# Where the high and low parts of the second weights stay before they are stored

## The chip, the cores and the metric

The kernel runs on one core of a Trainium2 chip. The metric is the device time of one execution in microseconds. Three runs of the kernel before took 868.1 us in the median, from 867.8 to 869.28.

## The reference

A retention layer (4 batches, 8 heads, 576 positions, head size 64) is followed by two MLPs on 2304 tokens of width 512, with 2048 hidden units each. The first has softplus, the second x * sigmoid(1.702 x). The MLP weights come as float64.

```python
ret = (q @ k.T / 8 * decay) @ v                  # per batch and head, causal
x = ret.transpose(0, 2, 1, 3).reshape(2304, 512)
x = softplus(x @ moe_w_in) @ moe_w_out
h = x @ moe2_w_in
out = (h * sigmoid(1.702 * h)) @ moe2_w_out
```

## The kernel before

**Precision.** Each float32 operand of a matmul is split into a high part (a cast to float32r) and a low part (the operand minus the high part). A product is three matmuls: high by high, low by high, high by low.

**Stages.** The work list of the first MLP runs over five token blocks (three batches of 512 tokens, a block "t" of the four batches' last 64 tokens each, and the last batch) and, in each, over 16 hidden blocks of 128. Between its matmuls `run_first` calls `side()`. Each call advances two Python generators by a rate: the retention of the next batch (`batch`) and one conversion of weights. So every engine's order of instructions is fixed when the program is built. The first weights are converted beside the first batch (`w1_gen`). From the second block on the generator is `w2_gen` at `W2RATE` 1.1, which converts the second MLP's weights in 32 pieces of 128 x 512 and stores them to DRAM. At the start of block "t" what is left of it is run out (L1108), the pools of that stage are closed, and `sums_steps` reads the whole weights back to build sums of quarters. In the second MLP (`run_second`, a seven-product scheme of Strassen-Winograd) the weights are loaded again as high and low halves from the DRAM tiles `kept_d`, `rest_d` and `sums_d`.

**One conversion step** (`convert`, L101). A weight arrives as two 32-bit words. ACT rescales the high word as a float into a tile `wa` (L110, "rebase"); VectorE keeps the sign (L115) and puts the bits together in two shift-or instructions (L130, L137); ACT casts the high part (L141 by the helper at L93); VectorE subtracts for the low part (L146 by the helper at L98). A `yield` stands between these, so each piece falls behind another matmul group in the queues. `begin(i)` for the second weights issues the read of piece i+2 on SP's queue (L576); `end(i, a)` is `w2_store`: it stores the two parts on SP's queue (L600) to one or two DRAM places, and the whole float piece on the GpSimd queue (L602). Then the next piece is rebased.

**Buffers.** The pool `wr` has two buffers of `wa` (4 KB per partition; the second weights use the first half) and three of the tag `raw64` (4 KB each), shared by the raw pieces that are read and by the `halves` tile:

```python
t = wr.tile([P, DM, 2], U32, tag="raw64", name="raw64", bufs=3)            # w2_read
w2_half["t"] = wr.tile([P, 2, DM], F32R, tag="raw64", name="halves", bufs=3)  # w2_place
```

A tile's buffer comes free when all its readers are done, a store from it included; the instruction that first writes the next tile in that buffer waits for that. Which free buffer a tile gets is settled when the program is built.

**SP's queue** holds, in the order of the program, the loads of k, q, v (L302) and of the ends (L306), the reads L576 and the stores L600. A DMA that waits holds up those behind it.

Of the kernel before, what the change touches and what calls it, by code (L numbers as in the profile page):

```python
# [7 lines left out]
F32 = mybir.dt.float32  # L8
F32R = mybir.dt.float32r
# [6 lines left out]
P = 128  # L16
# [9 lines left out]
N2 = 256  # L26
# [3 lines left out]
KEPT = [("in", "11"), ("in", "12"), ("in", "22"), ("out", "11"), ("out", "21"), ("out", "22")]  # L30
# [3 lines left out]
def kernel(  # L34
# [35 lines left out]
    nc = tc.nc  # L70
    B, _, NPAIR, _, KQV = kqv.shape
    H, D = 2 * NPAIR, P // 2
    NT, DM = out.shape
# [14 lines left out]
    def f32(t):  # L88
        return t.bitcast(F32)

    def hi(eng, dst, src):
        if eng == "a":
            nc.scalar.copy(dst, src)  # L93
        else:
            nc.vector.tensor_copy(dst, src)

    def lo(dst, src, h):
        nc.vector.tensor_tensor(out=dst, in0=src, in1=f32(h), op=ALU.subtract)  # L98


    def convert(n, ready, words, place, begin, end, early):  # L101

        def rebase(i):
            w = words(i)
            a = wr.tile([P, 2 * DM], F32, tag="wa", name="wa")[:, 0:w.shape[1]]
            nc.scalar.mul(a, w[:, :, 1].bitcast(F32), 2.0 ** -112)  # L110
            return w, a

        def sign(w):
            high = w[:, :, 1]
            nc.vector.tensor_single_scalar(out=high, in_=high, scalar=0x80000000, op=ALU.bitwise_and)  # L115

        nxt = None
        signed = set()
        for i in range(n):
            while nxt is None:  # L120
                if ready(i):
                    nxt = rebase(i)
                yield
            w, a = nxt
            nxt = None
            u = a.bitcast(U32)
            low, high = w[:, :, 0], w[:, :, 1]
            if i not in signed:
                sign(w)
            nc.vector.scalar_tensor_tensor(  # L130
                out=u, in0=u, scalar=3, in1=high, op0=ALU.logical_shift_left, op1=ALU.bitwise_or)
            begin(i)
            ahead = i + 1 < n and early(i + 1) and ready(i + 1)
            if ahead:
                nxt = rebase(i + 1)
            yield
            nc.vector.scalar_tensor_tensor(  # L137
                out=u, in0=low, scalar=29, in1=u, op0=ALU.logical_shift_right, op1=ALU.bitwise_or)
            yield
            h, l = place(i)  # L140
            hi("a", h, a)  # L141
            if ahead:
                sign(nxt[0])
                signed.add(i + 1)
            yield
            lo(l, a, h)  # L146
            end(i, a)
            if nxt is None and i + 1 < n and ready(i + 1):
                nxt = rebase(i + 1)
            yield  # L150

    def w_tile():
        return wp.tile([P, 2, 2, DM], F32R, tag="w", name="w")
# [87 lines left out]
    with tc.manual_schedule():  # L241
# [6 lines left out]
        kept_d = [dp.tile([P, 2, 4, N2], F32R, tag=f"kept_{i}", name=f"kept_{i}") for i in range(6 * NP // 4)]  # L248
        sums_d = {(j, s): dp.tile([P, 2, 4, N2], F32R, tag=f"sums_{s}{j}", name=f"sums_{s}{j}")
                  for j in range(NP) for s in ("in", "out")}  # L250
        rest_d = {(j, s): dp.tile([P, 2, 4, N2], F32R, tag=f"rest_{s}{j}", name=f"rest_{s}{j}")
                  for j in range(NP // 4) for s in ("in", "out")}
# [27 lines left out]
        with ExitStack() as consts, ExitStack() as right, ExitStack() as second:  # L280
            ac = consts.enter_context(tc.tile_pool(name="ac", bufs=1))
            ap = right.enter_context(tc.tile_pool(name="ap", bufs=2, side="right"))
            wr = right.enter_context(tc.tile_pool(name="wr", bufs=2, side="right"))
# [12 lines left out]
            halves = [slice(h * D, (h + 1) * D) for h in range(2)]  # L296
# [226 lines left out]
            for sv in svs[0] + svs[1]:  # L523
# [3 lines left out]
                out=mask[:, 0:4, :].rearrange("p (t u) j -> p t (u j)", u=2),  # L527
                in_=mask[:, 0:4, :].rearrange("p (t u) j -> p t (u j)", u=2), compare_op=ALU.is_ge, fill=0.0,
# [15 lines left out]

            made = {"f": 0}

            def w1_place(f):
                w1[f] = w_tile()
                return [w1[f][:, i].rearrange("p s n -> p (s n)") for i in range(2)]

            w1_gen = convert(
                NF, lambda f: (1, f) in raws, lambda f: raws.pop((1, f)), w1_place, lambda f: None,
                lambda f, a: made.update(f=f + 1), lambda f: f > 1)

# [24 lines left out]

            w2_half = {}  # L580

            def w2_place(i):
                w2_half["t"] = wr.tile([P, 2, DM], F32R, tag="raw64", name="halves", bufs=3)
                return w2_half["t"][:, 0], w2_half["t"][:, 1]

            def w2_store(i, a):

                j, o, s = i // 4, i // 2 % 2, ("in", "out")[i % 2]
                t = w2_half["t"].rearrange("p h (c n) -> p h c n", c=2)
                names = [(s, f"{o + 1}{n + 1}") for n in range(2)]  # L590
                n = 0
                while n < 2:
                    m = 1
                    if names[n] in KEPT:
                        m = 2 if n == 0 and names[1] in KEPT else 1
                        q = 6 * j + KEPT.index(names[n])
                        dst = kept_d[q // 4][:, :, q % 4:q % 4 + m, :]
                    else:
                        dst = rest_d[j // 4, s][:, :, j % 4:j % 4 + 1, :]
                    nc.sync.dma_start(out=f32(dst), in_=f32(t[:, :, n:n + m, :]))  # L600
                    n += m
                nc.gpsimd.dma_start(out=whole_d[j, s][:, o, :], in_=a)  # L602

            def w2_steps():

                w2_read(0)
                w2_read(1)
                for _ in range(8):
                    yield
                yield from convert(  # L610
                    2 * NF, lambda i: (2, i) in raws, lambda i: raws.pop((2, i)), w2_place,
                    lambda i: w2_read(i + 2), w2_store, lambda i: False)
# [601 lines left out]
```

## Time and profile before

| | |
|---|---|
| median of three runs | 868.1 us (867.8 to 869.28) |
| the profiled execution's own time | 867.41 us |
| its span | 865.7 us |
| TensorE busy | 847.3 us (98%) |
| VectorE busy | 577.5 us (67%) |
| ACT busy | 408.4 us (47%) |
| GpSimd busy | 97.1 us (11%) |
| mean busy share of the DMA queues of SP / GpSimd | 36.8% / 33.6% of 16 engines |

The times of matmuls are modelled and overlap, so a busy TensorE is not one at its peak. Waits are put down to the event that came last. A DMA's landing time counts from its issue.

### The profile page before, as it was taken

Reading aid. Unit: us, or ns where it says so; the run is one execution under the profiler, and the core shown is the slowest. Engines: PE = TensorE matmul, PEld = TensorE weight load, DVE = VectorE, ACT = ScalarE, POOL = GpSimd, SP = SyncE. Lnnn points to the kernel's source line nnn. Section 1 sums busy time; section 2 is a strip of 40 time slices with the busy share of each in tenths; the row PEclk is TensorE's granted clock in tenths of the full one; section 3 lists DMA queues with packets and bytes.
Section 4 is the critical chain, followed back from the end, with each engine's and each line's share of the span. In section 5 each row is a group of like instructions: output and inputs, shape, how many; then the busy total and the mean of one; then the engine's idle time right before and its main releaser. Section 6 shows DMA issues by size and latency. Waiting matters only on the chain.

```text
span 865.7 us, 15675 instructions
## 1 busy us (share of the span) xinstructions
PE 847.3 (98%) x6155; PEld 760.0 (88%) x6155; DVE 577.5 (67%) x1162; ACT 408.4 (47%) x809; POOL 97.1 (11%) x174
## 2 busy tenths in 40 slices
PE   8899999999999999999999999999999999999997
PEld 5678888888878778999888899999999999999997
DVE  5899964767567765577433467788778777866521
ACT  4655544344354433456333455465555555554321
POOL 4100001100110000101001121100011111001000
PEclk9999999999999999999999999999999999999999
DMA  9836531777869776599996596978697779776511
GB/s 362 346 130 219 210 110 62 231 273 268 287 227 300 244 234 237 209 368 334 384 368 209 180 348 240 319 297 291 243 319 282 262 265 336 270 262 223 204 68 25
DMA packets 62777, 217.30 MB, mean 251 GB/s; under 512 B 6384, under 2 KB 20848, under 8 KB 50416
## 3 DMA queue, kind: packets, MB, share of 16 engines
q1 hardware_dynamic: 45136, 111.96, 36.8%
q0 software_dynamic: 17568, 104.34, 33.6%
q8 instruction: 48, 0.79, 0.3%
q14 instruction: 25, 0.20, 0.1%
HBM read 157.56 MB, written 58.72 MB: 250 GB/s over the span
## 4 chain that ended last, share of the span: by engine, by line
PE 62%; issue 19%; DVE 9%; DMA 5%; ACT 3%; POOL 2%; POOLq 0%; SPq 0%; DVEq 0%; ACTq 0%
PE ph L765 15%; PE m L765 14%; PE ph L162 13%; PE y L162 12%; DMA kept<-halves 3%; PE y L765 3%; PE ps_h L331 2%; DMA xo<-x 1%; PE ps_s L383 1%; DVE wa L137 1%; POOL w L684 1%; DVE wa L130 1%; PE ps_y L331 1%; DVE w L98 1%; DMA sums_out<-sum_halves 1%
## 5 line engine op out<-in xcount | busy, mean ns | idle before, releaser
L162 PE MATMUL y<-gh,w 128*128 128x512 f32 (+1 forms) x640 | 196.6, 371 | 0.0
L162 PE MATMUL ph<-xh,w 128*128 128x512 f32 (+1 forms) x640 | 185.8, 374 | 5.3 <-ACT xh L93 2.0
L162 PEld LDWEIGHTS ph<-xh,w 128*128 128x128 f32 x640 | 115.3, 190 | 29.0 <-ACT xh L93 2.4
L162 PEld LDWEIGHTS y<-gh,w 128*128 128x128 f32 x640 | 117.1, 189 | 21.0
L162 PE MATMUL ph<-xl,w 128*128 128x512 f32 (+1 forms) x320 | 118.6, 371 | 0.2 <-DVE xl L98 0.2
L162 PE MATMUL y<-gl,w 128*128 128x512 f32 (+1 forms) x320 | 117.8, 368 | 0.0
L765 PE MATMUL m<-w,ga 128*128 128x256 f32 x768 | 117.3, 282 | 0.5 <-DVE yb L837 0.5
L98 DVE TENSOR_TENSOR gl<-g,gh 128x512 fp32r<-128x512 f32 (+1 forms) x80 | 51.0, 637 | 90.3 <-ACT gh L93 89.9
L765 PE MATMUL ph<-xo,w 128*128 128x256 f32 x768 | 105.8, 283 | 2.5 <-DVE ho L1031 1.1
L765 PE MATMUL ph<-xo_c,w 128*128 128x256 f32 x768 | 108.3, 283 | 0.0
L765 PEld LDWEIGHTS m<-w,ga 128*128 128x128 f32 x768 | 102.8, 190 | 1.1 <-PE ph L765 1.1
L765 PEld LDWEIGHTS ph<-xo,w 128*128 128x128 f32 x768 | 97.6, 189 | 4.1 <-DVE ho L1031 2.2
L765 PEld LDWEIGHTS ph<-xo_c,w 128*128 128x128 f32 x768 | 97.9, 188 | 1.4 <-DVE he L993 0.6
L210 ACT ACTIVATE g<-ph 128x512 f32<-128x512 f32 (+1 forms) x80 | 44.3, 553 | 115.0 <-PE ph L162 111.9
L765 PE MATMUL m<-w,gb 128*128 128x256 f32 x576 | 89.7, 282 | 0.0
L765 PEld LDWEIGHTS m<-w,gb 128*128 128x128 f32 x576 | 78.1, 191 | 0.0
L162 PEld LDWEIGHTS ph<-xl,w 128*128 128x128 f32 x320 | 60.8, 190 | 11.1 <-DVE xl L98 0.8
L162 PEld LDWEIGHTS y<-gl,w 128*128 128x128 f32 x320 | 60.4, 189 | 9.3
L93 ACT CAST halves<-wa 128x512 fp32r<-128x512 f32 x32 | 19.8, 619 | 78.8 <-DMA kept<-halves 31.5
L98 DVE TENSOR_TENSOR ga<-g,ga 128x512 fp32r<-128x512 f32 x72 | 47.0, 685 | 10.0 <-ACT ga L93 10.0
L93 ACT CAST ga<-g 128x512 fp32r<-128x512 f32 x72 | 44.7, 621 | 16.2 <-PE y L765 7.9
L93 ACT CAST gh<-g 128x512 fp32r<-128x512 f32 (+1 forms) x80 | 46.3, 578 | 2.4
(153 smaller groups left out, 1144.9 us busy)
## 6 DMA issues: line engine op xcount, KB each, us to landing
w<-sums_in POOLq DMA_DIRECT2D x32, 1024.0 KB, 5.6
w<-sums_out POOLq DMA_DIRECT2D x32, 1024.0 KB, 7.8
raw<-kqv SPq DMA_DIRECT2D x24, 512.0 KB, 4.5
w<-kept POOLq DMA_DIRECT2D x12, 1024.0 KB, 8.2
w_raw<-w_in SPq DMA_DIRECT2D x16, 512.0 KB, 7.0
w_raw<-w_out SPq DMA_DIRECT2D x16, 512.0 KB, 7.8
raw<-w_in SPq DMA_DIRECT2D x16, 512.0 KB, 4.5
raw<-w_out SPq DMA_DIRECT2D x16, 512.0 KB, 4.2
```

Of the source, the lines that this page charges most:

```text
L93: nc.scalar.copy(dst, src)
L98: nc.vector.tensor_tensor(out=dst, in0=src, in1=f32(h), op=ALU.subtract)
L130: nc.vector.scalar_tensor_tensor(out=u, in0=u, scalar=3, in1=high, op0=ALU.logical_shift_left, op1=ALU.bitwise_or)
L137: nc.vector.scalar_tensor_tensor(out=u, in0=low, scalar=29, in1=u, op0=ALU.logical_shift_right, op1=ALU.bitwise_or)
L162: nc.tensor.matmul(out_ap, l, r, start=first and i == 0, stop=last and i == k - 1)
L210: nc.scalar.activation(g, ph, AF.Softplus)
L331: nc.tensor.matmul(po[halves[h], at], l, rhs, start=clear[h], stop=True, skip_group_check=True)
L383: nc.tensor.matmul(ps[h][:, j], k[r, j], q[r, j], start=True, stop=True)
L684: nc.gpsimd.dma_start(out=where[i], in_=src)
L765: nc.tensor.matmul(out_ap, l, r, start=clear, stop=True, skip_group_check=True)
```

## The change

Three things change, all in the conversion of the second weights. The cast writes the high part into the second half of the piece's own `wa` tile. The low part is written over the first half of the raw piece, whose words have all been read by then. So there is no `halves` tile, and the three `raw64` buffers hold raw pieces only. High and low are then in two tiles, so `w2_store` issues its stores for each of them; the DRAM places stay as they were. The first weights' `w1_place` gets the new arguments and ignores them.

```diff
         def rebase(i):
             w = words(i)
-            a = wr.tile([P, 2 * DM], F32, tag="wa", name="wa")[:, 0:w.shape[1]]
-            nc.scalar.mul(a, w[:, :, 1].bitcast(F32), 2.0 ** -112)
-            return w, a
+            t = wr.tile([P, 2 * DM], F32, tag="wa", name="wa")
+            nc.scalar.mul(t[:, 0:w.shape[1]], w[:, :, 1].bitcast(F32), 2.0 ** -112)
+            return w, t
...
-            w, a = nxt
+            w, t = nxt
             nxt = None
+            a = t[:, 0:w.shape[1]]
...
-            h, l = place(i)
+            h, l = place(i, w, t)
...
-            def w1_place(f):
+            def w1_place(f, w, t):
...
-            def w2_place(i):
-                w2_half["t"] = wr.tile([P, 2, DM], F32R, tag="raw64", name="halves", bufs=3)
-                return w2_half["t"][:, 0], w2_half["t"][:, 1]
+            def w2_place(i, w, t):
+                w2_half["t"] = (t[:, DM:2 * DM].bitcast(F32R),
+                                w.rearrange("p n two -> p (n two)")[:, 0:DM].bitcast(F32R))
+                return w2_half["t"]
 
             def w2_store(i, a):
...
-                t = w2_half["t"].rearrange("p h (c n) -> p h c n", c=2)
                 names = [(s, f"{o + 1}{n + 1}") for n in range(2)]
-                n = 0
-                while n < 2:
-                    m = 1
-                    if names[n] in KEPT:
-                        m = 2 if n == 0 and names[1] in KEPT else 1
-                        q = 6 * j + KEPT.index(names[n])
-                        dst = kept_d[q // 4][:, :, q % 4:q % 4 + m, :]
-                    else:
-                        dst = rest_d[j // 4, s][:, :, j % 4:j % 4 + 1, :]
-                    nc.sync.dma_start(out=f32(dst), in_=f32(t[:, :, n:n + m, :]))
-                    n += m
+                for part, t in enumerate(w2_half["t"]):
+                    n = 0
+                    while n < 2:
+                        m = 1
+                        if names[n] in KEPT:
+                            m = 2 if n == 0 and names[1] in KEPT else 1
+                            q = 6 * j + KEPT.index(names[n])
+                            dst = kept_d[q // 4][:, part, q % 4:q % 4 + m, :]
+                        else:
+                            dst = rest_d[j // 4, s][:, part, j % 4:j % 4 + 1, :]
+                        nc.sync.dma_start(
+                            out=f32(dst), in_=f32(t[:, n * N2:(n + m) * N2]).rearrange("p (c n) -> p c n", c=m))
+                        n += m
                 nc.gpsimd.dma_start(out=whole_d[j, s][:, o, :], in_=a)
```

## Rows read from the trace of the kernel before

**Rows 1.** The page, busy time and share of the span by engine.

```profile
...
PE 847.3 (98%) x6155; PEld 760.0 (88%) x6155; DVE 577.5 (67%) x1162; ACT 408.4 (47%) x809; POOL 97.1 (11%) x174
...
```

**Rows 2.** Busy time by stage, seven slices from 145 to 347 us, their sum.

```profile
...
sum 202.00, PE 200.41 PEld 162.37 DVE 136.50 ACT 87.32 POOL 21.83; mean PE 28.63 PEld 23.20 DVE 19.50 ACT 12.47 POOL 3.12
```

**Rows 3.** Waits of PE, 145 to 347: waiter, released by, us in total, times, longest.

```profile
...
PE ph L162 <- ACT g L210: 1.0, 2, 0.7
PE ph L162 <- DVE xf L425: 0.4, 1, 0.4
PE ph L162 <- DVE xl L98: 0.2, 1, 0.2
```

**Rows 4.** Waits of ACT in the same stretch.

```profile
...
ACT g L210 <- PE ph L162: 37.2, 19, 5.5
ACT halves L93 <- DMA kept<-halves: 31.5, 10, 6.7
...
ACT halves L93 <- DMA rest_out<-halves: 14.4, 4, 4.9
...
```

**Rows 5.** Waits of SP's DMA queue in the same stretch.

```profile
...
SPq L576 <- DMA kept<-halves: 23.8, 9, 4.0
...
SPq L576 <- DVE wa L137: 14.9, 14, 2.2
...
```

**Rows 6.** The tile halves: duration in ns min/median/max, first and last start; landings.

```profile
...
L93 ACT CAST halves<-wa x32: 606/620/623, 151.6 to 341.7; 128x512 fp32r<-128x512 f32 x32
...
L600 SPq DMA_DIRECT2D kept<-halves x32: 513/525/799, 155.5 to 343.1; - x32
...
DMA to landing us min/median/max: 2.4/3.4/6.6
```

**Rows 7.** Line L756, the two stores of an x quarter in the second stage; landings.

```profile
...
L756 SPq DMA_DIRECT2D x<-x_hi x6: 319/320/448, 505.5 to 678.8; - x6
L756 SPq DMA_DIRECT2D x<-x_lo x6: 319/392/712, 506.2 to 679.5; - x6
...
DMA to landing us min/median/max: 2.0/2.6/11.2
```

**Rows 8.** The reads of raw second weights, L576: landings.

```profile
...
DMA to landing us min/median/max: 3.4/4.4/6.4
```

**Rows 9.** Timeline of PE around its four stalls; idle before and releaser in brackets.

```profile
243.85 0.50 PE L162 MATMUL ph<-xl,w 128*128 128x512 f32 x1 [0.17 <-DVE xl L98]
...
248.43 0.72 PE L162 MATMUL ph<-xh,w 128*128 128x512 f32 x2 [0.75 <-ACT g L210]
...
282.75 0.70 PE L162 MATMUL ph<-xh,w 128*128 128x512 f32 x2 [0.37 <-DVE xf L425]
...
311.88 0.73 PE L162 MATMUL ph<-xh,w 128*128 128x512 f32 x2 [0.30 <-ACT g L210]
```

**Rows 10.** Timeline of ACT: one rebase, three casts, the next rebase, a split.

```profile
205.75 0.66 ACT L110 ACTIVATE wa<-raw 128x512 f32<-128x512 f32 x1
...
239.63 0.62 ACT L93 CAST halves<-wa 128x512 fp32r<-128x512 f32 x1 [4.89 <-DMA rest_out<-halves]
...
277.66 0.62 ACT L93 CAST halves<-wa 128x512 fp32r<-128x512 f32 x1 [2.31 <-DMA kept<-halves]
...
310.71 0.62 ACT L93 CAST halves<-wa 128x512 fp32r<-128x512 f32 x1 [6.70 <-DMA kept<-halves]
...
312.38 0.66 ACT L110 ACTIVATE wa<-raw 128x512 f32<-128x512 f32 x1
...
346.79 1.32 ACT L93 CAST xh<-xt 128x256 fp32r<-128x256 f32 x4
```

**Rows 11.** Timeline of VectorE: two low parts and one shift-or.

```profile
211.22 0.69 DVE L98 TENSOR_TENSOR halves<-wa,halves 128x512 fp32r<-128x512 f32 x1 [2.06 <-ACT halves L93]
...
305.23 0.69 DVE L137 SCALAR_TENSOR_TENSOR wa<-raw,wa 128x512 uint32<-128x512 uint32 x1
...
342.39 0.69 DVE L98 TENSOR_TENSOR halves<-wa,halves 128x512 fp32r<-128x512 f32 x1
```

## The prediction

> **What bounds the kernel now.** Read the shares of the span first, then the busy time by stage, then who waits for whom, one engine at a time, in the stage that the change touches.
>
> TensorE is busy for 847.3 us, 98% of the span [rows 1]. So an edit on another engine can only give back the little that TensorE waits, or make it wait more. The second weights are converted between 148 and 343 us. In the stretch from 145 to 347 us TensorE is busy for 200.41 of 202 us, so all of its idle time there is 1.59 us [rows 2]. The waits of PE name the pieces: 1.0 us in two waits for a softplus on ACT (L210), 0.4 us for a VectorE evacuation (L425), 0.2 us for a split on VectorE (L98) [rows 3]. That is the whole of what a change in this stage can win by removing waits.
>
> ACT has far more waiting. In the same stretch the cast of the high parts (`halves<-wa`, L93) waits for a store of an earlier pair of halves to land: 31.5 us in ten waits and 14.4 us in four, together 45.9 us [rows 4]. The cast needs a free one of the three raw64 buffers, and the one it gets is that of the previous halves, still being stored. A store lands 3.4 us after issue in the median and 6.6 us at most; the casts run from 151.6 to 341.7 us, which is 190.1 / 31 = 6.13 us a step [rows 6]. So the chain cast, low part, store, next cast has little room in a step of 6.13 us: 0.62 for the cast, about 0.7 for the low part and up to 6.6 for the landing are 7.9 us. That is the wait that the change takes away.
>
> **The change part by part.** The first weights' conversion (L110 to L148, up to 124 us) issues the same instructions as before; the changed signature alone costs nothing there.
>
> *The high part goes into the second half of the wa tile.* The cast keeps its size, so 0.620 us, 32 times: no difference. It no longer asks for a raw64 buffer, so it starts when the second shift-or on VectorE (L137) ends. The wait is not gone altogether: wa has two buffers, and the rebase (L110) of step i+1 must now wait for the high part's store of step i-1 as well as for the whole store. But in ACT's order that rebase stands behind the cast of step i, and in some steps behind the softplus and its split too. What is late next is therefore the same landing, seen by a later instruction, with two steps (12.3 us) for its loop where there was one.
>
> How much of the 45.9 us reached TensorE? Three of its four stalls begin with such a wait. At 311.88 PE resumes 0.30 us late behind the softplus, which stands behind a cast at 310.71 that waited 6.70 us for a landing [rows 9, 10]; the shift-or that this cast really needs ran from 305.23 to 305.92 [rows 11], so the softplus could have run as soon as its matmuls were done. At 282.75 PE is 0.37 us late behind the evacuation L425; VectorE had stood for the cast at 277.66, which waited 2.31 us [rows 9, 10]. At 243.85 PE is 0.17 us late behind the split of the next batch, and ACT comes to that split after the cast at 239.63, which waited 4.89 us [rows 9, 10]. Sum of the three: 0.84 us. The fourth, 0.75 us at 248.43 [rows 9], follows a softplus that itself waits for PE; it is no work of the conversion and I leave it. As a stall also costs a slower first matmul or two, I bound the gain at 0.84 us from below and at the stage's 1.59 us from above, and take 1.0 us, near the three rows.
>
> *The low part goes over the raw piece.* Same operation, same size. All readers of the piece have run by then, so it waits for no buffer. The price moves to the reading of the raw pieces: the three buffers now go round among reads alone, so the read of step i+2 waits, at the head of SP's queue, until the low part of step i-1 has landed. Before, 14 of the reads waited only for the shift-or (14.9 us) and 9 for a landing of the 512 or 256 KB stores already (23.8 us, with a few more for the rest stores) [rows 5]. Reads of the first kind will go out later, by at most one landing, 3.4 to 6.6 us. Behind a held read on SP stand the loads of k, q, v and the stores of the same step. The stores cannot be ready earlier anyway, since they need that step's cast. The loads of k, q, v are issued with three buffers, two pairs ahead.
>
> Does a late read reach ACT? The loop over three steps is: a step's work from rebase to the end of the low part, 205.75 to 211.91 or 6.2 us with a landing wait of 2.1 us still in it [rows 10, 11]; a store's landing, 3.4 us; a second issue, about 0.3 us; a raw read's landing, 4.4 us [rows 8]. Sum 14.3 us, where three steps have 18.4 us. So it is hidden with 4.1 us to spare. With both landings at their largest (6.6 and 6.4) it is 19.5 us, over by 1.1 us; ACT's softplus waits for PE 37.2 us in 19 waits, 2.0 us each, and that slack takes it [rows 4]. Cost taken: 0; bounds 0 and the slower rival below.
>
> *High and low are stored apart.* 48 stores become 96 with the same bytes and the same runs (1 or 2 KB). An issue of both parts takes 0.525 us [rows 6]; one of a single part of 256 KB takes 0.320 us in the second stage [rows 7]. So SP spends 96 x 0.32 = 30.7 us where it spent about 48 x 0.525 = 25.2 us; at the old price for each it would be 50.4 us. The stage has 202 us, and SP mostly waits in it: hidden, 0 us, between +5 and +25 us on SP. In return the store of the high part no longer waits for the low part and leaves about 0.7 us earlier. A wait of the second store for the first, both in one DRAM tile and interleaved by partition, can be excluded by the nearest rows: the two stores of an x quarter are of that form, and `x<-x_lo` leaves at 506.2 us, 0.7 us after `x<-x_hi` at 505.5 us, although these stores take 2.0 us at least to land [rows 7].
>
> The Trainium skill speaks against this split: "DMA: Bandwidth & Descriptors", section "Rules for kernel authors", asks to coalesce many small transfers, and the section "Anatomy of one DMA" gives about 2.0 us of fixed cost to each. Paid in a row, 48 more transfers would be 96 us more on SP, about half of the stage, and rival C would be the forecast. The trace agrees with a fixed part in each landing, but shows that two stores overlap, so that the second adds its issue and not its landing [rows 7].
>
> **Sum.** Profiled execution: 867.41 us, a span of 865.7 and 1.71 around it. 867.41 - 1.0 + 0 + 0 = 866.4 us. That execution is 0.69 us under the median of the runs shown, 868.1, so for a median I add it back: 867.1 us.
>
> **The rivals.**
> *A. The wait only moves.* The rebase now waits for the same landing, and the softplus behind it is as late as before. For it: both are on ACT, one instruction apart in many steps. Against it: behind the cast at 310.71 the next rebase comes at 312.38 only, with the softplus and its split between them [rows 10]. Time 868.1 us, no change.
> *B. Everything idle in the stage goes, with the restarts.* The 1.59 us of idle time, and for each of the four stalls up to 0.2 us of slow first matmuls (an estimate from the 0.70 to 0.73 us that a pair takes there [rows 9]): 2.3 us, 865.8 us. For it: the pieces all lie close to conversion steps. Against it: the largest one waits for a softplus that waits for PE.
> *C. The raw ring becomes the bound (slower).* If the 96 stores or the queueing behind held reads lengthen the landings, the loop of three steps exceeds 18.4 us. Its point: store and read landing together above 18.4 - 6.2 - 0.3 = 11.9 us, against 7.8 us in the median and 13.0 at the largest. At 13.0 each three steps lose 1.1 us, over 31 steps 11.4 us; the low part ends at 343.08 and the next batch's split on ACT starts at 346.79 [rows 10, 11], so 3.7 us of it are covered and 7.7 us reach TensorE: 875.8 us. Against it: both landings at their largest in every step.
>
> **How the numbers follow.** Forecast 0.52, A 0.17, B 0.18, C 0.10, something else 0.03. A measurement of this kernel tells a change from none at about 0.2%, which is 1.7 us here: under 866.4 counts as faster, over 869.8 as slower. The forecast's own range is 866.3 to 867.8; it gives 0.46 to no change and 0.06 to faster. A goes to no change, B to faster, C to slower; of the rest 0.01 to faster and 0.02 to slower. So faster 0.25, same 0.63, slower 0.12. The range takes in B with 0.1% of scatter from below (864.9) and the near part of C, 2.9 us over the forecast, from above (870.0).
>
> **What would show it.** In the profile after: the waits of ACT's cast for landings gone, and in their place waits of `wa<-raw` (L110) for stores, well under 45.9 us in all. The stalls of PE at 243.85, 282.75 and 311.88 gone, that at 248.43 still there. Reads of raw pieces all waiting for a landing on SP, and no wait of ACT for a raw read above 2 us. 96 stores with issues near 0.32 us and landings no longer than before. The forecast is wrong if PE has new waits for L210 or for the splits in this stage, if the last low part ends later than 346 us, or if anything outside 148 to 347 us changes by more than 0.5 us.

## The result, and the profile after

The changed kernel took 880.53 us in the median of six runs (877.0 to 882.35), beside 869.12 us for the kernel before (867.8 to 871.32). The ratio is 1.0126, with a 95% interval from 1.0103 to 1.0148: slower by 11 us. The forecast was 867.1 us in a range up to 870.0.

The page of the changed kernel begins as follows.

```profile
span 880.4 us, 15762 instructions
...
PE 854.5 (97%) x6154; PEld 764.9 (87%) x6155; DVE 579.5 (66%) x1162; ACT 409.5 (47%) x809; POOL 96.1 (11%) x174
...
PEclk8899999999989999999999999999999999999999
...
```

Line numbers have moved by one to three: L93, L98, L110 and L115 stay, L130 is now L131, L137 is L138, L162 is L163, L210 is L211, L425 is L426, L576 is L577, L600 is L602, and the store of the whole piece, L602 before, is L605.

The profiled span is 14.7 us longer (880.4 for 865.7), but not all of it belongs to the change. The first rebase of the second weights starts at 152.2 us, 4.1 us later than the 148.1 us of before; the granted clock shows low slices in the first 50 us, where the two kernels issue the same instructions and the row of the kernel before shows none:

```profile
...
PEclk9999999999999999999999999999999999999999
...
```

A second profile of the changed kernel, below, starts at 148.5 us. So the stretch to compare runs from that rebase to the split of block "t" on ACT: 152 to 363 us after, 148 to 347 us before, 211 us for 199. What follows it is about 1.5 us shorter than before.

The busy time in slices of that stretch, a row of the changed kernel and the sum (columns: stretch, busy us and instructions of PE, PEld, DVE, ACT, POOL, then granted clock, DMA share, GB/s), and under it the same of the kernel before:

```profile
...
250.00:260.00 10.00, 7.33 (x28) 4.71 (x28) 5.95 (x10) 5.03 (x10) 0.54 (x1) 0.66 0.66 192
...
sum 211.00, PE 200.89 PEld 161.40 DVE 136.75 ACT 85.53 POOL 20.56; mean PE 22.32 PEld 17.93 DVE 15.19 ACT 9.50 POOL 2.28
```

```profile
...
250.00:260.00 10.00, 10.00 (x69) 8.12 (x68) 6.67 (x14) 4.67 (x10) 3.25 (x6) 1.00 0.73 245
...
sum 199.00, PE 197.41 PEld 159.88 DVE 135.21 ACT 84.66 POOL 20.42; mean PE 21.93 PEld 17.76 DVE 15.02 ACT 9.41 POOL 2.27
```

TensorE idles for 211.00 - 200.89 = 10.1 us where it idled for 1.6 us, and is busy for 200.89 where it was busy for 197.41 us with the same work. The second part, 3.5 us, I put down to the clock: after a stall of 4.39 us the slice from 250 to 260 us shows a granted clock of 0.66, a mix of the two levels (1.2 and 2.4 GHz), where that of before shows 1.00. Together 8.5 + 3.5 = 12.0 us is what the stretch has grown by.

Who waits in it now: PE [rows 3].

```profile
...
PE ph L163 <- ACT xh L93: 4.4, 1, 4.4
PE ph L163 <- DVE xf L426: 3.0, 3, 1.4
PE ph L163 <- ACT g L211: 2.3, 3, 1.1
PE ph L163 <- DVE xl L98: 0.4, 1, 0.4
```

ACT [rows 4]:

```profile
...
ACT wa L110 <- DMA kept<-wa: 41.1, 16, 5.0
ACT g L211 <- PE ph L163: 19.8, 10, 5.4
ACT wa L110 <- DMA rest_out<-wa: 16.9, 6, 4.4
```

And SP's queue [rows 5]:

```profile
...
SPq L577 <- DMA kept<-raw: 90.5, 22, 6.5
...
SPq L577 <- DMA rest_out<-raw: 23.5, 7, 4.9
...
SPq L577 <- DMA rest_in<-raw: 4.8, 2, 3.3
...
```

The reader is to see three things. The cast's 45.9 us of waits for landings are gone, as forecast, but the rebase (L110) has 58.0 us of them. VectorE stands for that rebase, 43.0 us where it stood 0.8 us. And SP's reads, which waited 23.8 us for `kept` landings and 32.0 us for landings in all, now wait 90.5 and 118.8 us. A step takes longer, and the stores land later; first the rebase in the listing of a tile, after and before, then the landings of the stores L602 [rows 6] and of the reads L577 [rows 8]:

```profile
...
L110 ACT ACTIVATE wa<-raw x32: 641/662/697, 152.2 to 358.3; 128x512 f32<-128x512 f32 x32
...
```

```profile
...
L110 ACT ACTIVATE wa<-raw x32: 641/669/693, 148.1 to 339.1; 128x512 f32<-128x512 f32 x32
...
```

```profile
...
DMA to landing us min/median/max: 2.3/4.5/7.0
```

```profile
...
DMA to landing us min/median/max: 3.6/4.3/7.0
```

From 152.2 to 358.3 us are 6.65 us a step; before, the rebases ran from 148.1 to 339.1 us, 6.16 us a step. A store's landing has gone from 3.4 to 4.5 us in the median.

How one thing leads to another shows in the queue of SP between two batches (start us, us, line, DMA). Each row `kept<-raw` or `rest_out<-raw` is a low part, each `<-wa` a high part:

```profile
...
232.05 0.33 SPq L577 DMA_DIRECT2D raw<-w_out  x1
...
232.95 0.38 SPq L602 DMA_DIRECT2D kept<-wa  x1
233.42 0.38 SPq L602 DMA_DIRECT2D kept<-raw  x1
239.76 0.33 SPq L577 DMA_DIRECT2D raw<-w_in  x1
240.18 0.66 SPq L602 DMA_DIRECT2D kept<-wa  x1
240.90 0.42 SPq L602 DMA_DIRECT2D kept<-raw  x1
245.50 0.33 SPq L577 DMA_DIRECT2D raw<-w_out  x1
...
```

And on ACT, with the idle time before each instruction and what ended it:

```profile
...
233.50 0.62 ACT L93 CAST wa<-wa 128x512 fp32r<-128x512 f32 x1 [0.80 <-DVE wa L138]
239.16 0.66 ACT L110 ACTIVATE wa<-raw 128x512 f32<-128x512 f32 x1 [5.04 <-DMA kept<-wa]
...
241.76 0.62 ACT L93 CAST wa<-wa 128x512 fp32r<-128x512 f32 x1 [0.81 <-DVE wa L138]
244.53 0.66 ACT L110 ACTIVATE wa<-raw 128x512 f32<-128x512 f32 x1 [2.15 <-DMA kept<-wa]
...
250.57 0.66 ACT L110 ACTIVATE wa<-raw 128x512 f32<-128x512 f32 x1 [1.66 <-DMA rest_out<-wa]
251.13 2.16 ACT L93 CAST xh<-xf 128x512 fp32r<-128x512 f32 x4
...
```

The cast at 233.50 is done at 234.12. Its store does not leave then: it leaves at 240.18, right behind a read that stood at the head of the queue from 233.80 until 239.76, waiting for the low part issued at 233.42. The store lands at about 244.5, and there the rebase two steps on has waited for it, 2.15 us. The stores of the next step leave behind the next read, 245.50, which again waited for the low part of 240.90. So one step is: read, stores, landing of the last store, next read. It takes 7.7 us from 232.05 to 239.76 and 5.7 us from there to 245.50. At 251.13 the split of the next batch comes to its turn on ACT behind a held rebase, and TensorE waits for it, where before it waited 0.17 us at that place [rows 9]:

```profile
...
251.79 0.92 PE L163 MATMUL ph<-xh,w 128*128 128x512 f32 x2 [4.39 <-ACT xh L93]
...
```

### The profile page after: what moved, and what is told of

The parts are those of the page before. It is cut to its first block, busy times and chain, and to the rows that moved or that the text cites. A ratio compares the mean times of both kernels' runs of the same rounds, so it can differ in the third digit from the quotient of the medians.

```text
span 880.4 us, 15762 instructions
## 1 busy us (share of the span) xinstructions
PE 854.5 (97%) x6154; PEld 764.9 (87%) x6155; DVE 579.5 (66%) x1162; ACT 409.5 (47%) x809; POOL 96.1 (11%) x174
## 4 chain that ended last, share of the span: by engine, by line
PE 71%; DMA 9%; issue 8%; DVE 7%; ACT 3%; SPq 1%; POOL 1%; ACTq 0%; POOLq 0%; DVEq 0%
PE ph L768 19%; PE m L768 16%; PE ph L163 15%; PE y L163 14%; DMA kept<-wa 4%; PE y L768 3%; PE ps_h L332 2%; DMA x<-x_lo 1%; DMA rest_out<-raw 1%; DMA w_raw<-w_out 1%; DVE wa L131 1%; DMA kept<-raw 1%; PE ps_s L384 1%; DVE wa L138 1%; DMA rest_out<-wa 1%
## 5 line engine op out<-in xcount | busy, mean ns | idle before, releaser
L163 PE MATMUL ph<-xh,w 128*128 128x512 f32 (+1 forms) x640 | 188.2, 378 | 13.2 <-ACT xh L93 6.3
L163 PE MATMUL y<-gh,w 128*128 128x512 f32 (+1 forms) x640 | 196.8, 371 | 0.0
L163 PEld LDWEIGHTS ph<-xh,w 128*128 128x128 f32 x640 | 116.2, 191 | 38.5 <-ACT xh L93 7.2
L163 PEld LDWEIGHTS y<-gh,w 128*128 128x128 f32 x640 | 117.3, 189 | 21.1
L163 PE MATMUL ph<-xl,w 128*128 128x512 f32 (+1 forms) x320 | 119.9, 375 | 0.4 <-DVE xl L98 0.4
L163 PE MATMUL y<-gl,w 128*128 128x512 f32 (+1 forms) x320 | 117.8, 368 | 0.0
L98 DVE TENSOR_TENSOR gl<-g,gh 128x512 fp32r<-128x512 f32 (+1 forms) x80 | 51.0, 637 | 83.8 <-ACT gh L93 83.6
L211 ACT ACTIVATE g<-ph 128x512 f32<-128x512 f32 (+1 forms) x80 | 44.1, 551 | 101.3 <-PE ph L163 98.3
L163 PEld LDWEIGHTS ph<-xl,w 128*128 128x128 f32 x320 | 61.4, 192 | 11.6 <-DVE xl L98 1.1
L163 PEld LDWEIGHTS y<-gl,w 128*128 128x128 f32 x320 | 60.5, 189 | 9.4
L98 DVE TENSOR_TENSOR ga<-g,ga 128x512 fp32r<-128x512 f32 x72 | 47.0, 685 | 9.1 <-ACT ga L93 9.1
L93 ACT CAST ga<-g 128x512 fp32r<-128x512 f32 x72 | 44.7, 621 | 15.4 <-PE y L768 7.9
L110 ACT ACTIVATE wa<-raw 128x512 f32<-128x512 f32 x32 | 21.3, 665 | 58.0 <-DMA kept<-wa 41.1
L93 ACT CAST gh<-g 128x512 fp32r<-128x512 f32 (+1 forms) x80 | 46.3, 579 | 2.4
```

The lines of the kernel that those rows point to most:

```text
L110: nc.scalar.mul(t[:, 0:w.shape[1]], w[:, :, 1].bitcast(F32), 2.0 ** -112)
L163: nc.tensor.matmul(out_ap, l, r, start=first and i == 0, stop=last and i == k - 1)
L211: nc.scalar.activation(g, ph, AF.Softplus)
```

## The experiments

Theory 1 is that loop on SP. Theory 2 is the number of stores. Theory 3 is that the two wa buffers are held until the high part has landed. In later runs theory 1 is split in two: 1a, the loop costs by itself; 1b, it costs only because the rebase also waits for a high part that is held behind the read. Ratios are to the kernel before, measured beside each kernel.

**The read behind the stores.** The loop is opened by moving one DMA in SP's order.

```diff
                 nc.gpsimd.dma_start(out=whole_d[j, s][:, o, :], in_=a)
+                w2_read(i + 2)
...
-                    lambda i: w2_read(i + 2), w2_store, lambda i: False)
+                    lambda i: None, w2_store, lambda i: False)
```

> The changed kernel with one edit: the read of raw piece i+2 is issued behind the stores of step i instead of at its begin, so no store stands behind a held read on SP. Theory 1 (SP's order: the stores of step i stand behind the read of piece i+2, which waits for the low part of step i-1 to land; so each step takes one landing and the issues): about 868 to 871 us, and ACT's waits of the rebase for stores of wa fall from 58 us to under 20. Theory 2 (96 stores instead of 48 on SP, whatever their order): 877 to 882. Theory 3 (two wa buffers held until the high part has landed): 877 to 882, waits of the rebase stay near 58 us.

Measured: 868.19 us, ratio 1.0011 (0.9992 to 1.003). The storage is that of the changed kernel, and so are the 96 stores and the wa buffers; the price is gone, as far as the interval tells. The waits of ACT in the conversion's stretch:

```profile
...
ACT wa L110 <- DMA raw<-w_out: 14.7, 8, 3.3
ACT wa L110 <- DMA raw<-w_in: 11.3, 8, 3.6
...
```

No rebase waits for a store of wa any more. It waits 26.0 us for raw reads instead, which now leave later. Little of that reaches TensorE, whose waits in the stretch come to 3.7 us, for 10.1 us in the changed kernel and 1.6 us before. Theories 2 and 3, as causes by themselves, are out.

**The stores on the GpSimd queue.**

```diff
-                        nc.sync.dma_start(
+                        nc.gpsimd.dma_start(
                             out=f32(dst), in_=f32(t[:, n * N2:(n + m) * N2]).rearrange("p (c n) -> p c n", c=m))
```

> The changed kernel with the stores of both parts issued on the GpSimd queue, behind nothing but each other, the whole stores and the y stores; the reads stay on SP. Theory 1: 867 to 871, as no store stands behind a held read. Theory 2 (the count on SP): also 867 to 871. Theory 3 (wa held until the landing): 877 to 882 with waits of the rebase near 58 us.

Measured: 870.31 us, ratio 1.0028 (1.0006 to 1.005). The reads still wait for the low parts, but nothing that is ready stands behind them. It agrees with theory 1, and most of the price is gone; the rebase now waits 33 us for the whole stores on the GpSimd queue, so theory 3 is not measured purely by it.

**Only the stores split**, in the kernel before.

```diff
-                    nc.sync.dma_start(out=f32(dst), in_=f32(t[:, :, n:n + m, :]))
+                    for part in range(2):
+                        nc.sync.dma_start(out=f32(dst[:, part]), in_=f32(t[:, part, n:n + m, :]))
```

> The kernel before with one edit: each store of the halves tile is issued as two, high and low, so 96 stores; buffers and order as before. Theory 1: within 2 us of before (869), since the reads still wait mostly for the shift-or and no loop over SP closes. Theory 2: 877 to 882, as the changed kernel. Theory 3: as before, 869.

Measured: 869.63 us, ratio 1.0023 (0.9997 to 1.0049). The interval holds 1, so it was measured again:

> The kernel before with each store issued as two, once more with more rounds: its ratio was 1.0023, from 0.9997 to 1.0049. If 48 more stores cost something of themselves, 1.001 to 1.004 and clear of 1; if not, 1.000 within 0.002.

Measured: 871.83 us, ratio 1.0041 (1.0021 to 1.006). So 48 more stores do cost, 3.6 us by the ratio, in a kernel whose storage is untouched, and more than the 2 us that theory 1 had allowed. The waits of its ACT in the second run:

```profile
...
ACT halves L93 <- DMA kept<-halves: 40.7, 10, 6.2
...
ACT halves L93 <- DMA rest_out<-halves: 16.3, 4, 6.9
...
```

The cast waits 57.0 us for landings where it waited 45.9 us. The kernel before has a loop of its own (cast, low part, store, landing, next cast), and the second store of a pair sits in it.

**Only the high part moved.** The low part gets a tile of its own among the raw64 buffers.

```diff
-                w2_half["t"] = (t[:, DM:2 * DM].bitcast(F32R),
-                                w.rearrange("p n two -> p (n two)")[:, 0:DM].bitcast(F32R))
+                low = wr.tile([P, DM], F32R, tag="raw64", name="halves", bufs=3)
+                w2_half["t"] = (t[:, DM:2 * DM].bitcast(F32R), low)
```

> The changed kernel with only the high part moved (into wa); the low part gets a tile of its own in the raw64 buffers, as the halves had. Theory 1: in between, 870 to 876, since the reads again often wait for the shift-or only, and SP holds the stores less. Theory 2: 877 to 882. Theory 3: 877 to 882, waits of the rebase for stores of wa near 58 us.

Measured: 866.78 us, ratio 0.9991 (0.9969 to 1.0014). Theory 1 said 870 to 876, and that missed: this half of the change costs nothing at all, with 96 stores and with the same two wa buffers. Measured once more:

> The kernel with only the high part moved, once more with more rounds: its ratio was 0.9991, from 0.9969 to 1.0014. If moving the high part alone takes away what was forecast, 0.998 to 0.999; if it does nothing, 1.000; the ratio decides whether it is a kernel to keep.

Measured: 866.69 us, ratio 0.9976 (0.9956 to 0.9995). SP's waits in the second run:

```profile
...
SPq L577 <- DMA kept<-halves: 34.9, 12, 4.6
...
SPq L577 <- DVE wa L138: 13.0, 10, 2.4
...
SPq L577 <- DMA rest_out<-halves: 8.5, 5, 3.4
...
SPq L577 <- DMA rest_in<-halves: 3.1, 1, 3.1
...
```

The reads wait 34.9 + 8.5 + 3.1 = 46.5 us for landings and in ten cases for the shift-or only: they have other buffers to take, so the loop does not close at every step. TensorE's waits in the stretch are 0.7, 0.3 and 0.3 us, together 1.3 us for 1.6 before. That is a small gain like the one that the prediction had given to the whole change. Two intervals of which one holds 1 make it likely rather than sure, and that it comes by the forecast's mechanism is not shown: TensorE's waits fell by 0.3 us, the time by the ratio 0.9976 by 2 us.

**Both parts over the raw piece**, with 48 stores; the read is ahead of them. This closes the loop with no part in wa. Against the changed kernel, shortened:

```diff
-                w2_half["t"] = (t[:, DM:2 * DM].bitcast(F32R),
-                                w.rearrange("p n two -> p (n two)")[:, 0:DM].bitcast(F32R))
-                return w2_half["t"]
+                w2_half["t"] = w.rearrange("p n two -> p (n two)").rearrange("p (h n) -> p h n", h=2).bitcast(F32R)
+                return w2_half["t"][:, 0], w2_half["t"][:, 1]
...
-                for part, t in enumerate(w2_half["t"]):
+                t = w2_half["t"].rearrange("p h (c n) -> p h c n", c=2)
...
-                        nc.sync.dma_start(
-                            out=f32(dst), in_=f32(t[:, n * N2:(n + m) * N2]).rearrange("p (c n) -> p c n", c=m))
+                    nc.sync.dma_start(out=f32(dst), in_=f32(t[:, :, n:n + m, :]))
```

> Both parts are written over the raw piece, high in its first half and low in its second, and stored together in 48 stores as in the kernel before; wa holds only the float piece; the read of piece i+2 stays at the begin of step i, ahead of the stores of step i. Theory 1a (the loop over SP alone, landing of step i-1, read, stores of step i, landing, is enough to slow the conversion): 874 to 880, rebase waiting for raw reads that land late. Theory 1b (the loop costs only because the rebase also waits for a high part that is held behind the read): 867 to 871, as the rebase now waits for no store of this queue.

Measured: 871.77 us, ratio 1.0045 (1.0027 to 1.0062). It falls between the two expectations: by the time the loop alone costs, but a third of the changed kernel's price. The same with the read behind the stores:

> As the kernel with both parts over the raw piece, with the read of piece i+2 issued behind the stores of step i. Both theories: 866 to 869; it would show that the buffers were not at fault, as its storage is the tightest of all. If the late reads cost (the rebase waited 26 us for them in the kernel with the read behind the stores), 868 to 870.

Measured: 869.37 us, ratio 1.0004 (0.9986 to 1.0023). With the loop open the tightest storage of all costs nothing that shows.

**The read between the high part's stores and the low part's**, in the changed kernel.

```diff
                         n += m
+                    if part == 0:
+                        w2_read(i + 2)
                 nc.gpsimd.dma_start(out=whole_d[j, s][:, o, :], in_=a)
...
-                    lambda i: w2_read(i + 2), w2_store, lambda i: False)
+                    lambda i: None, w2_store, lambda i: False)
```

> The changed kernel with the read of piece i+2 between the high part's stores and the low part's stores of step i. Theory 1a: the low part's stores still stand behind a read that waits for the low part of step i-1, so the loop over SP is closed: 872 to 878. Theory 1b: 865 to 869, since the high part, for which the rebase waits, no longer stands behind the read; the rebase's waits for stores of wa fall from 58 us to under 15.

Measured: 868.76 us, ratio 1.0005 (0.9984 to 1.0025), as theory 1b said: a high part that is not held behind a read costs nothing. But this edit also leaves fewer stores in the loop, only the low part's, and the reads wait only 25.2 us for landings. The next run takes the two apart.

**Both parts over the raw piece, with 96 stores.** To the kernel with both parts over the raw piece and 48 stores:

```diff
-                    nc.sync.dma_start(out=f32(dst), in_=f32(t[:, :, n:n + m, :]))
+                    for part in range(2):
+                        nc.sync.dma_start(out=f32(dst[:, part]), in_=f32(t[:, part, n:n + m, :]))
```

> Both parts over the raw piece, the read ahead of the stores, and each store issued as two (96 stores): the loop over SP with the changed kernel's number of stores, but with no part in wa. Theory 1b (the rest of the price is the rebase waiting for a high part held behind the read): about 1.0045, as with 48 stores. The other reading (the loop over SP gets longer by the added stores, and that alone makes up the changed kernel's price): 1.009 to 1.013.

Measured: 881.56 us, ratio 1.0154 (1.0126 to 1.0181). Theory 1b falls: no rebase waits for a high part here, and the price is the changed kernel's or more. What differs from the kernel with 48 stores is the number of stores in the closed loop. First SP's waits of this kernel, then ACT's:

```profile
...
SPq L577 <- DMA kept<-raw: 102.9, 32, 7.6
...
SPq L577 <- DMA rest_out<-raw: 17.3, 11, 4.1
...
SPq L577 <- DMA rest_in<-raw: 4.8, 2, 4.1
...
```

```profile
...
ACT wa L110 <- DMA raw<-w_in: 29.2, 11, 6.8
ACT wa L110 <- DMA raw<-w_out: 26.8, 11, 4.8
...
```

The rebase here waits 56.0 us for raw reads that leave late; in the changed kernel it waited 58.0 us for high parts that leave late. Both are the same loop, seen at another instruction. The rebases of this kernel run from 151.1 to 361.7 us, 6.79 us a step.

**The changed kernel once more:**

> The changed kernel itself beside the two: 1.010 to 1.015 again. Its profile should show the same waits of the rebase for stores of wa (50 to 65 us) and of the reads for stores of the raw piece (100 to 125 us), whatever TensorE's clock was in the first 50 us.

Measured: 876.89 us, ratio 1.0097 (1.0065 to 1.0129), a little under what was expected, with 55.7 us of the rebase's waits and 116.3 us of the reads'.

```profile
...
L110 ACT ACTIVATE wa<-raw x32: 641/664/702, 148.5 to 352.6; 128x512 f32<-128x512 f32 x32
...
```

From 148.5 to 352.6 us are 6.58 us a step, with a start like that of before.

**Only the high part moved, and the read between.** An attempt at something better than both kernels.

```diff
                         n += m
+                    if part == 0:
+                        w2_read(i + 2)
...
-                    lambda i: w2_read(i + 2), w2_store, lambda i: False)
+                    lambda i: None, w2_store, lambda i: False)
```

> The kernel with only the high part moved, with the read between the high part's stores and the low part's. The rebase's waits for stores of wa (22 us) should fall under 12 us; time 0.996 to 0.998 of before. If those waits are hidden behind TensorE anyway, 0.9976 as without the edit.

Measured: 869.47 us, ratio 1.0011 (0.9996 to 1.0025): a miss. The waits of the rebase for stores of wa are gone, but 19.4 us of waits for raw reads, issued later, stand in their place. The best kernel of all is the one with only the high part moved.

Side by side, by what stands ahead of the stores on SP. The last column is the stretch from the first rebase of the second weights to the split of block "t" on ACT, in the one execution of each that was profiled:

| loop over SP | stores | kernel | ratio | stretch, us |
|---|---|---|---|---|
| open (read behind) | 48 | both over the raw piece | 1.0004 | 198.66 |
| open (read behind) | 96 | the change's storage | 1.0011 | 201.16 |
| none (stores on the GpSimd queue) | 96 | the change's storage | 1.0028 | 201.86 |
| low part's stores only | 96 | the change's storage, read between | 1.0005 | 199.89 |
| low part's stores only | 96 | only the high part moved, read between | 1.0011 | 199.37 |
| closed in part, by the buffers | 48 | before | 1 | 198.73 |
| closed in part, by the buffers | 96 | before, stores split | 1.0041 (first 1.0023) | 204.78 (first 201.36) |
| closed in part, by the buffers | 96 | only the high part moved | 0.9976 (first 0.9991) | 198.09 (first 197.54) |
| closed | 48 | both over the raw piece | 1.0045 | 200.59 |
| closed | 96 | the change | 1.0126 (again 1.0097) | 210.84 (again 208.60) |
| closed | 96 | both over the raw piece | 1.0154 | 215.44 |

The stretch leaves out the start, which differs by up to 4.7 us between these profiles (the first rebase starts at 148.1 to 152.8 us). By it the closed loop costs 9.9 to 16.7 us with 96 stores, but 1.9 us with 48, less than the 2.4 us of the open loop with 96: that the loop costs with 48 stores rests on the times alone, and it is the loop and the added stores together that make the price.

## Why the prediction was wrong

**What held.** TensorE's small idle time in the stage before, the cast's waits going, and waits of the rebase in their place, though 58.0 us of them where well under 45.9 us were expected. That there was a gain to be had is made likely by the kernel with only the high part moved, 0.9976 where 1.0 us had been forecast (0.9988).

**What failed: the step on the low part.** It saw that the read of piece i+2 would stand at the head of SP's queue until the low part of step i-1 had landed, and named the stores of the same step among what stands behind it. Then it dismissed them: "The stores cannot be ready earlier anyway, since they need that step's cast." The trace shows a store ready at 234.12 and issued at 240.18. The need of the cast does not bind, because the read leaves only when a store has landed, 6.3 and 4.6 us after its issue in the rows above, and the cast comes in that time. With the stores held, the next landing cannot begin, and the next read waits for it. So the loop is one step long: landing of the last store, the read's issue, the stores' issues. The prediction had priced a loop over three steps, 14.3 us of 18.4, and found 4.1 us to spare; the right sum from its own rows was, for one step, 3.4 (landing) + 0.33 (read) + about 1.0 (stores) = 4.7 us in the median and 7.9 us with the largest landing, against 6.13 us. That leaves 1.4 us in the median and nothing at the largest. In the run, behind a read just released, the landing was 4.5 us in the median and each of three stores took 0.42 us to issue: 4.5 + 0.33 + 1.26 = 6.1 us, the whole of a step of 6.13 us.

**And the step on the stores apart.** 48 more stores were priced as SP time, hidden, 0 us. In a closed loop each of them is a part of every step's length. The issues also cost more than taken, 0.42 us in the median for 0.32. Split stores alone took 1.0041 (first 1.0023) in the old storage, and with the loop closed the step from 48 to 96 stores is that from 1.0045 to 1.0154.

**Rival C** came nearest and got a chance of 0.10. It said that the ring of raw pieces becomes the bound, at 875.8 us. Its condition, longer landings by the 96 stores or by queueing behind held reads, was met; its point was wrong. It wanted store and read landings of 11.9 us together; 4.5 + 4.3 = 8.8 us sufficed, because the loop that closes has no read's landing in it.

The Trainium skill has a sentence that bears on this, in "DMA: Bandwidth & Descriptors", section "Anatomy of one DMA": a semaphore wait happens at the issuing sequencer before dispatch, and the DMA engines only consume their queues. The trace agrees: the read of 239.76, while it waited, held back a store behind it that was ready 6.1 us before it left. The rule of the Trainium skill on small transfers (same page, section "Rules for kernel authors"), which the prediction weighed and set aside, pointed the right way, but not by the prediction's sum of 2.0 us for each added transfer: with the loop open 96 stores took 1.0011. Nor was bandwidth missing: the mean busy share of the DMA engines from 145 to 240 us is 0.71, where it was 0.77. The figure of 2.0 us stands in that section for DMAs that GpSimd issues; these stores leave on SP's queue, where the shortest landing was 2.4 us before and 2.3 us after.

**How it reached TensorE.** The forecast took 2.0 us of slack for each softplus on ACT. But the loop does not cost one wait; it slows all steps, from 6.16 to 6.65 us, while the order of instructions is fixed by the program. The engines fall behind that order until TensorE waits 4.39 us for the next batch's split, and its granted clock is low after the stall (0.66 from 250 to 260 us). That the clock's part is 3.5 us is worked out from busy times, not tried by a run.

**What stays open.** Why a landing takes longer behind a read was not tried. Why two kernels with a loop closed in part and 96 stores differ (1.0041 and 0.9976) was not tried beyond their waits. In the first the cast itself waits for both stores of a pair; in the second only the low part's tile and, two steps on, the rebase do. A fourth raw buffer might open the loop as well; that was not tried, as the pool has no room for 4 KB more per partition.

## What to carry to other kernels

Before a buffer is reused in place, list each queue in order and ask of every DMA that will wait: what ready work stands behind it, and does the thing it waits for need that work? If yes, the loop's length is one landing plus all issues between, once per step, and every added DMA counts in it, however idle the queue looks. Moving the held DMA behind the ready ones can open the loop at no cost in memory: here one moved read brought the ratio from 1.0126 to 1.0011, some 10 us.

## What the runs showed of the hardware

A store that is issued right behind a 512 KB read on the same queue lands later. The medians of all stores L601/L602 were 4.5, 4.8 and 4.8 us in the three kernels with the closed loop, where a read just released stands ahead of them, and 3.3 and 3.4 us in the two with the read behind; in the others that store on SP they lie from 3.3 to 4.6 us. The listings of the two kernels with both parts over the raw piece and 48 stores, first with the read ahead, then with the read behind:

```profile
...
DMA to landing us min/median/max: 2.5/4.8/7.2
```

```profile
...
DMA to landing us min/median/max: 2.5/3.4/5.3
```

That is 1.4 us for the same stores and bytes, with nothing but the order on the queue changed. The changed kernel with the read between shows it within one kernel: its high parts leave ahead of the read, its low parts behind it. Size and median landing of those stores that take 256 KB:

```profile
...
kept<-wa SPq DMA_DIRECT2D x16, 256.0 KB, 3.7
kept<-raw SPq DMA_DIRECT2D x16, 256.0 KB, 5.1
...
```
